# An attention block and a gated feed-forward block in one kernel: the first batch masked by matrix multiplications, the loads and the first stages reordered

## The chip, the cores and the metric

The kernel runs on one core of one Trainium2 chip. The metric is the device time of one execution in microseconds, lower is better. The engines of the core work side by side, each through its own queue of instructions in order: TensorE (PE, matrix multiplications), VectorE (DVE), ScalarE (ACT), GpSimd (POOL) and SyncE (SP, here used only to issue DMAs). DMAs are also issued from POOL's queue and, at the start, from ACT's.

## The reference

```python
def _attn_ref(q, k, v, beacon_k, beacon_v):      # B, H, S, D = 8, 8, 576, 64; 16 beacon rows
    k_all = np.concatenate([beacon_k, k], axis=2)
    v_all = np.concatenate([beacon_v, v], axis=2)
    scores = scale * np.matmul(q, k_all.transpose(0, 1, 3, 2))
    causal[:, Nb:] = np.triu(np.ones((S, S), dtype=bool), k=1)   # beacons are never masked
    scores = np.where(causal, -1000000000.0, scores)
    scores = scores - scores.max(-1, keepdims=True)
    a = np.exp(scores)
    a /= a.sum(-1, keepdims=True) + 1e-09
    return np.matmul(a, v_all)

def _moe_ref(x, w_gate, w_val, w_out):           # x: 4608 x 512; 512 x 1536 twice; 1536 x 512
    g = x @ w_gate
    silu = g * (1.0 / (1.0 + np.exp(-g)))
    val = x @ w_val
    return silu * val @ w_out
```

The attention output of all heads, 4608 rows (tokens) of 512, is the input `x` of the feed-forward block.

## The kernel before

**Attention.** The 8 heads of a batch are worked in 4 pairs. For a pair, K and Q stand transposed in bf16 (`kT`, `qT`). `scores1` and `scores2` each multiply one half of the causal blocks for both heads into two PSUM tiles `s_ps` (8 multiplications of up to 496 columns in `scores2`, 4 in `scores1`), ACT takes the exponential of each tile into a tile `p` in SBUF, and POOL sets the masked entries of `p` to zero with `affine_select` (2 of them in `scores1`, 4 in `scores2`). `pv` multiplies `p` with V for one head (15 small multiplications), and DVE divides by the sum (`rec`, `x`). A pair is thus two score halves and two `pv`, and `pv` of a pair runs one step after its scores.

**Feed-forward.** Tokens go in 9 chunks of 512. A *unit* (`gv_unit`, in the schedule `G`) is 8 multiplications of 512 columns for 128 of the 1536 hidden columns, then tanh on ACT (`th`) and two DVE operations (`u`, `hT`); a chunk has 12 units. The projection of a chunk is 48 multiplications (`out_steps`, in the schedule `F(n)` for n of them): 4 output tiles of 12 each, and after the twelfth DVE copies the tile (`o_sb`) and SP writes it out.

**PSUM.** `big` has three tiles and serves scores and units in turn: whoever asks for a tile waits until the tile three requests earlier has been read (exponential for `s_ps`, `hT` for `gv_ps`). `att` and `outp` are one tile each, for `pv`, transposes and projections.

**Loads and transposes.** Batches below `NPE` = 3 get K and Q as f32 through SP's queue (for the first two pairs of batch 0, Q through ACT's), are cast by DVE (K) and by DVE or ACT (Q), and are transposed on PE (`transpose_pair`, five multiplications and a DVE copy). Later batches are loaded by POOL's queue, whose DMAs cast to bf16 on the way, and transposed by DMA (`dma_transposes`). V and the weights `wg`, `wv` (4 loads each of 384 hidden columns) and `wo` (two loads) come by POOL's casting loads; `pool_todo` hands such loads to POOL in small groups behind the masks of a score half. `x` is transposed on PE for batch 0 (`x_transpose_pair`) and by DMA on SP's queue for the others.

**Order.** It is written by hand and every engine keeps it. Batch 0 has attention alone. Then each pair's scores and `pv` stand between three units, from batch 2 on with 12 projection steps as well: `G scores1 pv F(6) scores2 G pv F(6) G`. Units of chunk j start after batch j+1's second pair has begun. What is left after batch 7 is units and projections alone.

Of the kernel before, what the change touches and what calls it, by code (L numbers as in the profile page):

```python
# [24 lines left out]
NPE = 3  # L25
# [21 lines left out]
def kernel(  # L47
# [30 lines left out]
    o_pool = ctx.enter_context(tc.tile_pool(name="o", bufs=3))  # L78
# [23 lines left out]
    def tiles(t):  # L102
        return t[:].rearrange("p (c h d) -> p c h d", c=NKT, h=H)
# [76 lines left out]
    def transpose_pair(dst, src, n, b, m, pool, tag):  # L180
# [28 lines left out]
    def scores(b, m, which, spec, cols):  # L209
        s = [big.tile([P, 1024], FP32, name="s_ps", tag="big") for _ in range(2)]  # L210
        for t, col, q0, n in spec:
            for hh in range(2):
# [5 lines left out]
                    start=True,  # L218
                    stop=True,
                )  # L220
        for hh in range(2):
# [3 lines left out]
            )  # L225

# [25 lines left out]
    def pv(b, m, hh):  # L252
# [3 lines left out]
        o_ps = att.tile([P, NKT, 68], FP32, name="pv_ps", tag="att")  # L256
# [19 lines left out]
    def x_transpose_pair(b, m, pool, tag):  # L276
# [5 lines left out]
        nc.vector.tensor_copy(xT[:, m, S * b : S * b + S], t_ps[:])  # L282
# [76 lines left out]

    for i in range(2):  # L360
# [10 lines left out]
    make_identity(nc, ident)  # L371
    for load in v_loads(0, 0, 4) + v_loads(0, 4, 8):
# [5 lines left out]

    v1, v2 = v_loads(1, 0, H), v_loads(2, 0, H)
    pool_todo += [[], [], w_loads(0), [], v1[0:3], [], [], v1[3:6]]  # L380
    pool_todo += [w_loads(1), w_loads(2), w_loads(3), [lambda: load_wo(0), lambda: load_wo(1)]]
    pool_todo += [v2[0:3], v2[3:6]]

    steps = [(b, m) for b in range(B) for m in range(NPAIR)]
    end = (B, 0)

    def at(s):
        return steps[s] if 0 <= s < len(steps) else end

    def load_qk_f32(b, h0, h1):  # L390
        load_k_f32(nc.sync, b, h0, h1)
        load_q_f32(nc.sync, b, h0, h1)
# [6 lines left out]
    cast_q(0, 1)  # L399
    load_qk_f32(1, 0, 4)  # L400
# [131 lines left out]
```

## Time and profile before

| | us |
|---|---|
| median of three runs (423.41 to 428.55) | 425.1 |
| the profiled execution | 422.91 |
| its span, first to last instruction | 421.2 |

PE is busy in 377.5 us of the span (90%), DVE in 236.5, ACT in 175.2, POOL in 160.2. A matmul's busy time counts from its start to a modelled end, and the next one starts before that end, so what a multiplication costs in a row is read from start to start and not from the busy figure. The granted TensorE clock is 1.00 of full speed in most of the span and 0.50 in three short stretches.

### The profile page before, as it was taken

How to read it: one execution, taken by the hardware profiler on the slowest of the kernel's cores; microseconds unless marked ns; L12 is line 12 of the kernel's file. 1: busy time of each engine (PE TensorE's matmuls, PEld its weight loads, DVE VectorE, ACT ScalarE, POOL GpSimd, SP SyncE). 2: the span in 40 equal slices, each digit the busy share in tenths (PEclk: the TensorE clock that was granted, in tenths of full speed). 3: DMA queues.
4: the chain of work that ended last, by engine and by line, in shares of the span. 5: the costliest groups of instructions: out<-in, count | busy, mean ns of one | idle time of the engine just before them, and what ended most of it. 6: DMA issues, size and time to landing. Idle time of an engine off the chain costs nothing.

```text
span 421.2 us, 7286 instructions
## 1 busy us (share of the span) xinstructions
PE 377.5 (90%) x2736; PEld 182.2 (43%) x2780; DVE 236.5 (56%) x458; ACT 175.2 (42%) x253; POOL 160.2 (38%) x317
## 2 busy tenths in 40 slices
PE   2756998956998799999999999999999999999996
PEld 1435453422444344444444444444444544444442
DVE  3643766741655455555555555555555664585551
ACT  1536555531445345445555555444555211232210
POOL 8546465390617561846193629261112100000000
PEclk9995998996999999999999999999999999999999
DMA  9999999799868986999499929991310131000012
GB/s 162 152 199 143 188 206 182 84 140 127 74 94 56 170 93 82 94 172 114 64 103 181 125 51 121 150 135 39 75 34 25 41 93 51 25 25 26 25 50 101
DMA packets 169427, 42.89 MB, mean 102 GB/s; under 512 B 159152, under 2 KB 164784, under 8 KB 169392
## 3 DMA queue, kind: packets, MB, share of 16 engines
q0 software_dynamic: 92144, 15.56, 49.0%
q1 hardware_dynamic: 74848, 26.28, 31.6%
q10 hardware_dynamic: 2400, 0.59, 0.7%
q8 instruction: 22, 0.36, 0.4%
q14 instruction: 13, 0.11, 0.1%
HBM read 38.27 MB, written 9.44 MB: 113 GB/s over the span
## 4 chain that ended last, share of the span: by engine, by line
PE 63%; DVE 11%; DMA 11%; another core or an unknown queue 5%; ACT 4%; SPq 2%; issue 2%; ACTq 0%; DVEq 0%
PE gv_ps L301 29%; PE o_ps L330 19%; PE s_ps L214 7%; PE pv_ps L260 6%; DMA q<-in_q_dram 6%; DVE u L312 4%; DVE hT L315 4%; ACT th L310 4%; DMA xT<-x 3%; SPq L289 2%; PE t_ps L185 1%; DMA k<-in_k_dram 1%; DVE qT L186 1%; DVE o_sb L339 1%
## 5 line engine op out<-in xcount | busy, mean ns | idle before, releaser
L312 DVE SCALAR_TENSOR_TENSOR u<-th,gv_ps 128x512 f32<-128x512 f32 x108 | 74.3, 688 | 133.3 <-ACT th L310 133.0
L310 ACT ACTIVATE th<-gv_ps 128x512 f32<-128x512 f32 x108 | 64.4, 597 | 178.9 <-PE gv_ps L301 157.1
L232 POOL TENSOR_SCALAR_AFFINE_SELECT p<-p 128x256 bf16<-128x256 bf16 x192 | 66.6, 380 | 165.7 <-ACT p L223 165.2
L301 PE MATMUL gv_ps<-xT,wg 128*128 128x512 bf16 x418 | 111.6, 383 | 9.8 <-DMA xT<-x 7.8
L223 ACT ACTIVATE p<-s_ps 128x720 bf16<-128x720 f32 (+1 forms) x128 | 103.8, 869 | 37.1 <-PE s_ps L214 36.6
L301 PE MATMUL gv_ps<-xT,wv 128*128 128x512 bf16 x424 | 110.2, 381 | 0.1
L330 PE MATMUL o_ps<-wo,hT 128*128 128x512 bf16 x410 | 101.7, 379 | 1.4 <-DVE o_sb L339 0.4
L315 DVE SCALAR_TENSOR_TENSOR hT<-gv_ps,u 128x512 bf16<-128x512 f32 x108 | 74.7, 691 | 3.7
L214 PE MATMUL s_ps<-qT,kT 64*128 64x96 bf16 (+5 forms) x384 | 48.2, 305 | 18.7 <-ACT p L223 9.1
L301 PEld LDWEIGHTS <-wv 128*128 128x128 bf16 x432 | 42.5, 98 | 51.7 <-issue 1.3
L301 PEld LDWEIGHTS <-wg 128*128 128x128 bf16 x432 | 40.1, 99 | 55.9 <-issue 10.7
L330 PEld LDWEIGHTS <-hT 128*128 128x128 bf16 x432 | 39.0, 98 | 40.4 <-issue 0.6
L260 PEld LDWEIGHTS <-p 128*128 128x128 bf16 x960 | 38.0, 102 | 20.0 <-issue 12.5
L260 PE MATMUL pv_ps<-vb,p 128*128 128x65 bf16 x960 | 43.0, 199 | 1.8 <-DVE kT L186 1.1
L214 PEld LDWEIGHTS <-kT 64*128 64x128 bf16 x384 | 15.8, 98 | 50.8 <-issue 43.9
L114 POOL DMA_DIRECT2D vb<-in_v_dram x45 | 36.8, 831 | 0.3 <-issue 0.2
L269 DVE TENSOR_TENSOR x<-pv_ps,rec 128x320 bf16<-128x320 f32 x64 | 31.5, 492 | 2.2
L339 DVE COPY o_sb<-o_ps 128x512 f32<-128x512 f32 x36 | 24.8, 689 | 11.3 <-PE o_ps L330 11.1
L114 POOL DMA_DIRECT2D kb<-in_k_dram x25 | 21.2, 873 | 0.0
L114 POOL DMA_DIRECT2D qb<-in_q_dram x25 | 21.2, 887 | 0.0
L268 DVE RECIPROCAL rec<-pv_ps 128x5 f32<-128x5 f32 x64 | 12.1, 190 | 6.4 <-PE pv_ps L260 6.2
L185 PE MATMUL t_ps<-ident,kb 128*128 128x128 bf16 (+1 forms) x60 | 7.3, 265 | 6.7 <-DVE kb L169 6.4
(30 smaller groups left out, 74.6 us busy)
## 6 DMA issues: line engine op xcount, KB each, us to landing
out_dram<-o_sb SPq DMA_DIRECT2D x36, 256.0 KB, 2.2
vb<-in_v_dram POOLq DMA_DIRECT2D x21, 128.0 KB, 5.7
q<-in_q_dram SPq DMA_DIRECT2D x20, 128.0 KB, 7.5
qb<-in_q_dram POOLq DMA_DIRECT2D x20, 128.0 KB, 5.5
k<-in_k_dram SPq DMA_DIRECT2D x24, 96.0 KB, 4.9
kb<-in_k_dram POOLq DMA_DIRECT2D x15, 128.0 KB, 4.4
wg<-in_moe_w_gate_dram POOLq DMA_DIRECT2D x4, 384.0 KB, 8.1
wv<-in_moe_w_val_dram POOLq DMA_DIRECT2D x4, 384.0 KB, 10.1
```

What stands on the lines that cost most here:

```text
L114: eng.dma_start(dst[p0 : p0 + n, c, h0:h1, 0:D], src[b, h0:h1, r : r + n, :].rearrange("h j d -> j h d"))
L214: nc.tensor.matmul(s[hh][:, col : col + n], lhsT=kT[b % 2][r, m, P * t : P * t + P], rhs=qT[b % 2][r, m, q0 : q0 + n], start=True, stop=True,)
L223: nc.scalar.activation(p[:, cols[0] : cols[1]], s[hh][:, cols[0] : cols[1]], ACT.Exp, scale=0.125)
L232: nc.gpsimd.affine_select(out=ap, in_=ap, compare_op=ALU.is_ge, fill=0.0, base=base, pattern=pattern, channel_multiplier=-1,)
L260: nc.tensor.matmul(o_ps[:, c, 0 : D + 1], lhsT=pt[2 * (m % 2) + hh][w][:, col : col + P], rhs=vb[b % 2][:, t, h, 0 : D + 1], start=(t == 0 ...
L269: nc.vector.tensor_tensor(out=xs[b][:, :, D * h : D * h + D], in0=o_ps[:, :, 0:D], in1=rec[:].to_broadcast([P, NKT, D]), op=ALU.mult,)
L301: nc.tensor.matmul(ps[:, TOK * half : TOK * half + TOK], lhsT=w[:, kk, P * f : P * f + P], rhs=xT[:, kk, r : r + TOK], start=(kk == 0), st ...
L310: tanh = nc.scalar.activation(th[:], ps[:, 0:TOK], ACT.Tanh, scale=0.5)
L312: nc.vector.scalar_tensor_tensor(out=u[:], in0=th[:], scalar=1.0, in1=ps[:, 0:TOK], op0=ALU.add, op1=ALU.mult)
L315: nc.vector.scalar_tensor_tensor(out=hTs[j][:, f, :], in0=ps[:, TOK:1024], scalar=0.5, in1=u[:], op0=ALU.mult, op1=ALU.mult)
L330: nc.tensor.matmul(st["o"][:], lhsT=hTs[j][:, f, P * i : P * i + P], rhs=wo[:, f, :], start=(f == 0), stop=(f == NF - 1),)
L339: nc.vector.tensor_copy(o_sb[:], st["o"][:])
```

## The change

The diff does six things.

1. In batch 0 the mask is added before the exponential, on PE: a triangular tile `below` of -30000 is multiplied with the identity and added onto the scores, 4 extra multiplications in `scores1` and 6 in `scores2`; POOL's selects are left out there. From batch 1 on they stay.
2. Only the first pair's Q of batch 0, and K of batch 0, are loaded as f32. The rest of Q in batch 0 and all of K and Q of batch 1 come by POOL's casting loads; batch 2 is transposed by DMA (`NPE` = 2).
3. POOL issues 49 loads in a row at the start: Q and V of batch 0, `w` parts 0 and 1, K and Q of batch 1, `w` parts 2 and 3, `wo`, V of batch 1.
4. Eleven multiplications of 512 columns on zeros are run by PE at the start.
5. Chunk 0's 12 units follow batch 0's attention directly, with batch 1's PE transposes between them (their copies on ACT). Batch 1's attention then runs beside the projection of chunk 0; its `x` is transposed on PE too. Chunk 1's first two units are split into parts by `gv_mm` and `gv_act`.
6. From batch 2 on a step is `scores1 pv F(3) scores2 pv F(3) G G G F(6)` (the table `fill` has what batches 2, 3 and 4 leave out of it); DMA transposes are handed out five per step. `o_pool` has 6 buffers in place of 3.

```diff
-NPE = 3
+NPE = 2
-    o_pool = ctx.enter_context(tc.tile_pool(name="o", bufs=3))
+    o_pool = ctx.enter_context(tc.tile_pool(name="o", bufs=6))
...
+        if b == 0:
+
+            for hh in range(2):
+                for t, col, q0, n in spec:
+                    if t or not which:
...
+                        nc.tensor.matmul(
+                            s[hh][:, c0 : c0 + w],
+                            lhsT=below[:],
+                            rhs=ident[:, lo : lo + w],
+                            start=False,
+                            stop=t != 2,
+                        )
...
+            if b == 0:
+                continue
...
+    warm(11, TOK)
...
-    for h in range(0, H, 2):
-        load_k_f32(nc.sync, 0, h, h + 2)
-        load_q_f32(nc.scalar if h < 4 else nc.sync, 0, h, h + 2)
...
+    load_k_f32(nc.sync, 0, 0, 2)
+    load_q_f32(nc.scalar, 0, 0, 2)
+    for m in range(1, NPAIR):
+        load_k_f32(nc.sync, 0, 2 * m, 2 * m + 2)
+    first = q_loads(0, 2, 6) + v_loads(0, 0, 4) + q_loads(0, 6, H) + v_loads(0, 4, H)
+    first += w_loads(0) + w_loads(1) + k_loads(1, 0, H) + q_loads(1, 0, H) + w_loads(2) + w_loads(3)
+    first += [lambda: load_wo(0), lambda: load_wo(1)] + v_loads(1, 0, H)
...
+    for m in range(NPAIR):
+        scores1(0, m)
+        if m < last:
+            transpose_k(0, m + 1, outp, "outp")
+        if m > 1:
+            pv(0, m - 1, 0)
+        scores2(0, m)
+        if m < last:
+            transpose_q(0, m + 1, outp, "outp")
...
+    for _ in range(3):
+        G()
+    for m in range(NPAIR):
+        transpose_k(1, m, outp, "outp", nc.scalar)
+        G()
+        transpose_q(1, m, att, "att", nc.scalar)
+        if m != 1:
+            G()
...
+    fq += out_steps(0, one_bank)
+    for m in range(NPAIR):
+        scores1(1, m)
+        if m >= 2:
+            F(1)
+            x_transpose_pair(1, m - 2, att, "att")
+            F(2)
+        if m:
+            pv(1, m - 1, 0)
+        F(3)
+        scores2(1, m)
+        F(2)
+        if m:
+            pv(1, m - 1, 1)
+        F(1)
...
+    steady = [([], [3], [], [3, g, g, g, 6])] * 4
+    short = ([], [3], [], [3, g, g, g])
+    fill = {
+        2: [([6], [3], [], [3, g, g, g]), ([], [], [], [g, g, g]), ([], [], [], [g, g]), ([], [], [], [g, g])],
+        3: [([], [3], [], [21]), ([], [3], [], [3]), ([], [], [], [g, g, g]), ([], [], [], [g, g, g])],
+        4: [steady[0], short, short, steady[0]],
+    }
...
+                pool_todo += group(loads, 2 if b == 3 else 3)
+            n = fill.get(b, steady)[m]
+            run(n[0])
+            scores1(b, m)
+            if prev:
+                pv(*prev, 0)
+            run(n[1])
+            scores2(b, m)
+            run(n[2])
+            if prev:
+                pv(*prev, 1)
```

On POOL, early in batch 0, the masks of the first score halves stand between V's loads and the first weight loads before the change (`p` are the exponentials, `vb` is V, `wg` and `wv` are the weights):

```order
L114 DMA vb_94<-in_v_dram 128x4x64 x3
L114 DMA vb_94<-in_v_dram 80x4x64
L232 AFFINE_SELECT p_0_100<-p_0_100 128x2x128
L232 AFFINE_SELECT p_1_102<-p_1_102 128x2x128
L232 AFFINE_SELECT p_0_101<-p_0_101 128x2x128
L232 AFFINE_SELECT p_0_101<-p_0_101 128x96
L232 AFFINE_SELECT p_1_103<-p_1_103 128x2x128
L232 AFFINE_SELECT p_1_103<-p_1_103 128x96
L232 AFFINE_SELECT p_2_104<-p_2_104 128x2x128
L232 AFFINE_SELECT p_3_106<-p_3_106 128x2x128
L154 DMA wg<-in_moe_w_gate_dram 128x4x384
L154 DMA wv<-in_moe_w_val_dram 128x4x384
```

After the change POOL's queue holds, behind the second weight part, batch 1's K (`kb`) and Q (`qb`) and the third weight part:

```order
L120 DMA kb_94<-in_beacon_k_dram 16x8x64
L120 DMA kb_94<-in_k_dram 112x8x64
L120 DMA kb_94<-in_k_dram 128x8x64 x3
L120 DMA kb_94<-in_k_dram 80x8x64
L120 DMA qb_92<-in_q_dram 128x8x64 x4
L120 DMA qb_92<-in_q_dram 64x8x64
L161 DMA wg<-in_moe_w_gate_dram 128x4x384
L161 DMA wv<-in_moe_w_val_dram 128x4x384
```

No select stands among the 49 loads, and the third weight part has moved behind two whole tensors of batch 1.

On ACT, where batch 0 ends, batch 1's exponentials (`p0_...`, `p1_...`) and Q casts stood around the first three tanh of chunk 0 (`th`):

```order
L223 ACTIVATE p1_0_101<-s_ps_587 128x720
L223 ACTIVATE p1_1_103<-s_ps_588 128x720
L176 ACTIVATE qb1_91<-q32_88 128x4x128
L176 ACTIVATE qb1_91<-q32_88 64x128
L310 ACTIVATE th_659<-gv_ps_650 128x512
L310 ACTIVATE th_673<-gv_ps_664 128x512
L310 ACTIVATE th_687<-gv_ps_678 128x512
L223 ACTIVATE p0_2_104<-s_ps_692 128x960
L223 ACTIVATE p0_3_106<-s_ps_693 128x960
```

In the changed kernel the last exponentials of batch 0 are followed by three copies of transposed `x`, five tanh, and the first copy of batch 1's transposed K:

```order
L259 ACTIVATE p1_2_106<-s_ps_495 128x720
L259 ACTIVATE p1_3_108<-s_ps_496 128x720
L189 ACTIVATE xT_112<-xt_ps_555 128x576
L189 ACTIVATE xT_112<-xt_ps_584 128x576
L189 ACTIVATE xT_112<-xt_ps_593 128x576
L356 ACTIVATE th_606<-gv_ps_533 128x512
L356 ACTIVATE th_615<-gv_ps_581 128x512
L356 ACTIVATE th_629<-gv_ps_620 128x512
L356 ACTIVATE th_643<-gv_ps_634 128x512
L356 ACTIVATE th_657<-gv_ps_648 128x512
L201 ACTIVATE kT1_100<-t_ps_662 128x592
L356 ACTIVATE th_678<-gv_ps_669 128x512
```

Batch 1's first exponential now comes 20 rows after batch 0's last, behind all twelve tanh of chunk 0.

On DVE, one step of the later batches read before (`rec` and `x` after each `pv`, `o_sb` after a projection tile, `u` and `hT` after each unit):

```order
L268 RECIPROCAL rec_3440<-pv_ps_3424 128x5
L269 TENSOR_TENSOR x_3293<-pv_ps_3424,rec_3440 128x5x64
L339 COPY o_sb_3449<-o_ps_3371 128x512
L312 SCALAR_TENSOR_TENSOR u_3482<-th_3480,gv_ps_3471 128x512
L315 SCALAR_TENSOR_TENSOR hT_3378<-gv_ps_3471,u_3482 128x512
L268 RECIPROCAL rec_3501<-pv_ps_3485 128x5
L269 TENSOR_TENSOR x_3293<-pv_ps_3485,rec_3501 128x5x64
L312 SCALAR_TENSOR_TENSOR u_3522<-th_3520,gv_ps_3511 128x512
L315 SCALAR_TENSOR_TENSOR hT_3378<-gv_ps_3511,u_3522 128x512
L312 SCALAR_TENSOR_TENSOR u_3540<-th_3538,gv_ps_3529 128x512
L315 SCALAR_TENSOR_TENSOR hT_3378<-gv_ps_3529,u_3540 128x512
```

and reads now:

```order
L306 RECIPROCAL rec_3847<-pv_ps_3831 128x5
L307 TENSOR_TENSOR x_3708<-pv_ps_3831,rec_3847 128x5x64
L306 RECIPROCAL rec_3885<-pv_ps_3869 128x5
L307 TENSOR_TENSOR x_3708<-pv_ps_3869,rec_3885 128x5x64
L389 COPY o_sb_3891<-o_ps_3814 128x512
L358 SCALAR_TENSOR_TENSOR u_3906<-th_3904,gv_ps_3895 128x512
L361 SCALAR_TENSOR_TENSOR hT_3894<-gv_ps_3895,u_3906 128x512
L358 SCALAR_TENSOR_TENSOR u_3920<-th_3918,gv_ps_3909 128x512
L361 SCALAR_TENSOR_TENSOR hT_3894<-gv_ps_3909,u_3920 128x512
L358 SCALAR_TENSOR_TENSOR u_3934<-th_3932,gv_ps_3923 128x512
L361 SCALAR_TENSOR_TENSOR hT_3894<-gv_ps_3923,u_3934 128x512
```

Both `pv` come first, the copy of the projection tile stands ahead of the three units, and the last `hT` of a step is followed by the `rec` of the next step's first `pv`.

## Rows read from the trace of the kernel before

**Rows 1.** Busy time by stretch; columns: busy us and count per engine, granted clock, DMA.

```profile
0.00:43.02 43.02, 24.47 (x260) 16.11 (x261) 19.92 (x69) 19.52 (x27) 27.05 (x56) 0.88 1.21 165
43.02:166.12 123.10, 105.48 (x838) 51.48 (x850) 68.91 (x136) 56.82 (x84) 59.69 (x115) 0.96 1.11 127
166.12:330.50 164.38, 161.76 (x1228) 75.28 (x1249) 96.26 (x176) 80.90 (x112) 73.46 (x147) 1.00 0.87 97
330.50:421.20 90.70, 85.83 (x417) 39.35 (x423) 51.41 (x78) 17.91 (x30) 0.00 (x0) 1.00 0.14 48
```

**Rows 2.** Waits of PE from 0 to 166 us; columns: total us, times, longest us.

```profile
PE s_ps L214 <- ACT p L223: 9.1, 6, 6.9
PE gv_ps L301 <- DMA xT<-x: 7.8, 2, 5.9
```

**Rows 3.** Timeline of one step in batch 3; columns: start us, us, engine, line, operation.

```profile
147.12 0.69 DVE L315 SCALAR_TENSOR_TENSOR hT<-gv_ps,u 128x512 bf16<-128x512 f32 x1
147.39 1.03 PE L214 MATMUL s_ps<-qT,kT 64*128 64x496 bf16 x4
148.36 0.63 PE L260 MATMUL pv_ps<-vb,p 128*128 128x65 bf16 x15
148.82 1.46 PE L330 MATMUL o_ps<-wo,hT 128*128 128x512 bf16 x6
...
154.12 1.03 PE L301 MATMUL gv_ps<-xT,wg 128*128 128x512 bf16 x4
...
155.84 1.03 PE L301 MATMUL gv_ps<-xT,wg 128*128 128x512 bf16 x4
...
157.67 1.03 PE L214 MATMUL s_ps<-qT,kT 64*128 64x496 bf16 x4
```

**Rows 4.** Timeline of PE at a first score half with no wait before it.

```profile
104.32 0.58 PE L214 MATMUL s_ps<-qT,kT 64*128 64x496 bf16 x4
104.83 0.63 PE L260 MATMUL pv_ps<-vb,p 128*128 128x65 bf16 x15
```

**Rows 5.** Timeline of batch 0's second and third pair.

```profile
14.58 0.98 PE L214 MATMUL s_ps<-qT,kT 64*128 64x496 bf16 x4 [0.55 <-DVE qT L186]
...
19.98 0.98 PE L214 MATMUL s_ps<-qT,kT 64*128 64x496 bf16 x4 [0.59 <-DVE qT L186]
```

**Rows 6.** Groups by line, 166.12 to 330.5 us; columns: busy us, mean ns, idle before.

```profile
L223 ACT ACTIVATE p<-s_ps 128x960 bf16<-128x960 f32 x32 | 29.3, 968 | 4.0 <-PE s_ps L214 4.0
...
L232 POOL TENSOR_SCALAR_AFFINE_SELECT p<-p 128x256 bf16<-128x256 bf16 x64 | 26.5, 421 | 90.5 <-ACT p L223 90.2
L223 ACT ACTIVATE p<-s_ps 128x720 bf16<-128x720 f32 x32 | 22.9, 768 | 10.2 <-PE s_ps L214 10.2
...
L114 POOL DMA_DIRECT2D vb<-in_v_dram x15 | 12.7, 855 | 0.1
...
L232 POOL TENSOR_SCALAR_AFFINE_SELECT p<-p 128x96 bf16<-128x96 bf16 x32 | 9.0, 283 | 0.0
```

**Rows 7.** Timeline of PE: a `pv` in batch 0, a transpose of Q in batch 1.

```profile
17.77 1.03 PE L260 MATMUL pv_ps<-vb,p 128*128 128x65 bf16 x15
...
53.41 0.52 PE L185 MATMUL t_ps<-ident,qb 128*128 128x128 bf16 x5
```

**Rows 8.** DMA queues from 133 to 137 us; columns: packets, MB, share of 16 engines.

```profile
q0 software_dynamic: 3831, 0.48, 189.6%
```

**Rows 9.** The same from 85 to 97 us, beside DMA transposes.

```profile
q0 software_dynamic: 7577, 0.96, 140.6%
```

**Rows 10.** The same from 46 to 54 us, while weights and f32 rows load.

```profile
q0 software_dynamic: 1546, 1.16, 92.2%
```

**Rows 11.** Timeline of POOL's first loads, and of DVE beside them.

```profile
2.21 3.61 POOL L114 DMA_DIRECT2D vb<-in_v_dram  x5
...
6.39 3.60 POOL L114 DMA_DIRECT2D vb<-in_v_dram  x5
...
6.86 1.04 DVE L178 CAST qb<-q 128x512 bf16<-128x512 f32 x2
```

More of the change, by code (lines that the diff above doesn't have):

```diff
@@ L111, in spans @@
             )
+    loaded = {}
     def rows(eng, dst, src, b, h0, h1, c, p0, r, n):
-        eng.dma_start(
+        if src is not v and src is not beacon_v:
+            key = b, src is not q, c
+            loaded[key] = loaded.get(key, 0) + 1
+        return eng.dma_start(
             dst[p0 : p0 + n, c, h0:h1, 0:D], src[b, h0:h1, r : r + n, :].rearrange("h j d -> j h d")
@@ L357, in F, with warm @@
                 fq.pop(0)()
+    make_identity(nc, ident)
+    nc.gpsimd.memset(below[:], 0.0)
+    nc.gpsimd.affine_select(
+        out=below[:],
+        in_=below[:],
+        compare_op=ALU.is_ge,
+        fill=-30000.0,
+        base=0,
+        pattern=[[-1, P]],
+        channel_multiplier=1,
+    )
+    nc.vector.memset(pt[3][1][:], 0.0)
+    idle = big.tile([P, 1024], FP32, name="idle_ps", tag="big")
+    def warm(n, cols):
+        for _ in range(n):
+            nc.tensor.matmul(
+                idle[:, 0:cols], lhsT=pt[3][1][:, 0:P], rhs=pt[3][1][:, 0:cols], start=True, stop=True
+            )
+    warm(11, TOK)
     for i in range(2):
@@ L376, in group @@
         return [loads[i : i + n] for i in range(0, len(loads), n)]
[L379 to L392, printed above, removed]
+    last = NPAIR - 1
     cast_k(0, 0)
-    cast_q(0, 0)
+    cast_q(0, 0, nc.scalar)
     transpose_k(0, 0, outp, "outp")
@@ new lines @@
+    while gq:
+        G()
+    k2, q2 = k_loads(2, 0, H), q_loads(2, 0, H)
+    for load in k2[0:2] + q2[0:1]:
+        load()
+    for c in range(NKT):
+        pool_todo.append(([k2[c + 2], q2[c + 1]] if c + 1 < NKT else []) + dma_transposes(2)[2 * c : 2 * c + 2])
+    fq += out_steps(0, one_bank)
[13 more added lines that the diff above has]
+        F(1)
@@ new lines @@
+    for load in v_loads(2, 0, H):
+        load()
+    gv_mm(1, 0, 0, last - 1)
+    pv(1, last, 0)
+    F(2)
+    x_transpose_pair(1, last - 1, att, "att")
+    F(2)
+    pv(1, last, 1)
+    gv_mm(1, 1, 0, last - 1)
+    gv_mm(1, 0, last - 1, last)
+    x_transpose_pair(1, last, att, "att")
+    F(2)
+    gv_mm(1, 1, last - 1, last)
+    for f in range(2):
+        gv_mm(1, f, last, KD)
+        gv_act(1, f)
+    gq += [(1, f) for f in range(2, NF)]
+    kq3 = k_loads(3, 0, H) + q_loads(3, 0, H)
@@ new lines, with run @@
+    for load in kq3[0:6]:
+        load()
+    def run(n):
+        for k in n:
+            if k == "G":
+                G()
+            else:
+                F(k)
+    g = "G"
+    steady = [([], [3], [], [3, g, g, g, 6])] * 4
[5 more added lines that the diff above has]
+    }
@@ new lines @@
+    todo = []
+    prev = None
+    for b in range(2, B):
+        for m in range(NPAIR):
+            if m == 2 and b > 2:
+                gq += [(b - 1, f) for f in range(NF)]
+                fq += out_steps(b - 2, one_bank) if b > 3 else []
+            if m == 0 and b + 1 < B:
+                loads = kq3[6:] + [lambda: None] if b == 2 else []
+                if b + 2 < B:
+                    loads += k_loads(b + 2, 0, H) + q_loads(b + 2, 0, H)
+                else:
+                    pool_todo += [[], []]
+                loads += v_loads(b + 1, 0, H)
+                pool_todo += group(loads, 2 if b == 3 else 3)
+            n = fill.get(b, steady)[m]
+            run(n[0])
@@ L481 @@
+            if b == 2 and m == 3:
+                fq += out_steps(1, one_bank)
+            if m == (b == 2) and b + 1 < B:
+                todo = dma_transposes(b + 1)
+            for _ in range(5):
+                if todo:
+                    todo.pop(0)()
+            prev = (b, m)
     G()
```

176 lines of the change are left out of this document (76 added, 100 removed).

## The prediction

> **What bounds the kernel now.** I read the busy time by stretch first [rows 1]. From 166.12 us on PE is the bound: 161.76 of 164.38 us in batches 4 to 7, and behind them only units and projections. Before that it is not: 24.47 of 43.02 us until the first unit, 105.48 of 123.10 us in the next stretch. In those 166 us PE stands idle for 36 us, and part of the rest runs at half clock (0.88 and 0.96 granted). The waits say for whom [rows 2]: 9.1 us for exponentials, 6.9 of them one wait in which batch 1's f32 Q had not come, and 7.8 us for the transposed `x`. So the early part is held by loads and by the order, the late part by PE's own work. In the late part I then read one step [rows 3]: it lasts 157.67 - 147.39 = 10.28 us (164.38 / 16 = 10.27 over the sixteen steps, [rows 1]), of which a unit is 155.84 - 154.12 = 1.72, one 512-column multiplication so 0.215, a `pv` 148.82 - 148.36 = 0.46. The first score half takes 148.36 - 147.39 = 0.97 there, against 104.83 - 104.32 = 0.51 where it need not wait [rows 4]: its second tile is the one of the unit just before the last, and its `hT` ends only at 147.12 + 0.69 = 147.81.
>
> **How I sum.** At 166.12 us the kernel before has 78 units, 354 projection multiplications and 16 pairs to go (counted in the code). The changed kernel has the same left when batch 4 begins. So I need the time T at which that is, and what the rest costs. Prices, all from rows: a unit 1.72; a pair 2 x 0.46 for `pv`, 0.51 for the first score half and an estimated 0.40 for the second (720 columns against 960), 1.83; a pair's exponentials 2 x 0.97 + 2 x 0.77 = 3.47 on ACT; its masks 4 x 0.42 + 2 x 0.28 = 2.25 on POOL; a load of a tensor's 128 rows 0.86 on POOL [rows 6]; a PE transpose of a pair 0.52 [rows 7].
>
> **Batch 0 (until units 0 and 1 are done): 32 us.** Batch 0's second pair begins at 14.58 and its third at 19.98 [rows 5], 5.40 us apart, while ACT alone would need 3.47. Removed: POOL's masks and DVE's Q casts, which lie on the way from one pair to the next. Added: 10 mask multiplications a pair. No row shows them; nothing is the lower bound, since ACT's 3.47 can cover them, and 10 x 0.52 / 5 = 1.0 us, the transposes' price, the upper. I take them inside a pace of 4.5 us, between 3.47 and 5.40. K's f32 loads are first in SP's queue as before, so the second pair stays at 14.5; the fourth begins at 23.5, its exponentials end at 27, and its `pv`, three `x` transposes and what is left of two units take 5 us more.
> What the row shows of the loads that move to POOL: five loads took 3.61 us before DVE's casts begin and 3.60 beside them, 0.72 each [rows 11]. The Trainium skill, page "SBUF — State Buffer", section "SBUF: two separate sides", says that a DMA issued from GpSimd is held up while DVE runs a fast copy or cast, because its descriptors cannot be written. By that rule the four K casts of batch 0 would each hold a load up, by 0.4 to 0.5 us, and the sum would be 2 us higher; the row speaks against it here.
>
> **Chunk 0: until 55.7.** 10 units are 17.2, eight transposes at most 4.2, together 21 us, so 53. Are the weights there? POOL needs 0.65 to 0.72 for each of the 22 half loads ahead [rows 11], so `w` parts 0 and 1 are issued from 17 us on. Weight packets (768 B, 1024 a part pair) passed at 1546 / 8 = 193 a us with f32 rows beside them [rows 10]; without those I take 230. Small packets (one row of 64 values; 9344 for batch 1's K and Q) passed at 3831 / 4 = 958 a us alone [rows 8] and 7577 / 12 = 631 beside transposes [rows 9]. So parts 0 and 1 are in by 28, K and Q by 38, part 2 by 42.5, part 3 by 47, `wo` by 55, V of batch 1 by 60. Unit 6 is due at 39.8 and waits 2.7 us for part 2; the later units are then late enough.
>
> **Batch 1 beside projection 0: until 82.** PE's work is 4 x 1.83, 36 x 0.215, four `x` transposes of 0.52 and two units of chunk 1: 20.6 us. The first `pv` would come at 59 and waits for V until 60.5. Behind that POOL is late: 8 loads x 0.86 stand between the masks of the first two pairs, 9.0 + 6.9 = 16 us of POOL work that can only begin with the exponentials; I walked it step by step and get 4 us of waits of `pv` for masks. 20.6 + 1.5 + 4 = 26.1, say 26.3 with seams.
>
> **Batch 2: until 112, batch 3: until 142.** Batch 2 has 12 projection steps, 10 units and 4 pairs on PE, 27.2 us, and on POOL 23 loads and 24 masks, 19.8 + 9.0 = 28.8, after 12 further loads (10 us) queued in front. POOL is the bound by a little, and in three steps the second score half waits about 1 us for the last unit's tile, since no projection stands between: 30. Batch 3: 30 x 0.215 + 6 x 1.72 + 4 x 1.83 = 24.1 on PE, 17 x 0.86 + 9.0 = 23.6 on POOL behind what batch 2 left; waits for masks of 0.7 and 2.5, for a tile 1.1, seams 1: 30. T = 142, against 166.1: **24 us won**. With every wait of mine at zero T is 125 (32, 53, 73.6, 100.8, 124.9).
>
> **The rest.** In the new step six projection multiplications (1.3 us) stand between the third unit and the next scores, so the tile is free in time: 0.46 of the 10.27 go, and up to 0.24 of seams (10.27 less 3 x 1.72, 12 x 0.215, 1.83 and 0.46). The stall could only move to `o_sb`; but the projection tile ends with the second `F(3)`, ahead of three units, and its copy hides under 5.2 us of them. I take 9.72, between 9.57 and 10.27: 16 x 0.55 = 8.8 less 1.4 for three short steps of batch 4, whose tile wait stays at 0.45. The last stretch is the same work, 90.70. 164.4 - 7.4 + 90.7 = 247.7. Span 142 + 247.7 = 389.7; with the 1.7 us around the span (422.91 - 421.2) 391.4, against 422.91. The profiled execution is 0.5% below the median of 425.1, so I say **392** for the median.
>
> Costed at nothing: the eleven first multiplications (PE has nothing else to do before the first K comes; at half clock they are 11 x 0.43 = 4.7 us), the ACT copies of batch 1 (ACT has one tanh per unit there), the DMA transposes of batch 2 on SP (needed at 83, issued from 64 on), the six `o_sb` buffers, which cover output writes queued behind transposes that wait for loads.
>
> **Rivals.**
> - *My waits do not happen* (0.14). For it: every one is a few us and hangs on a rate. Against: POOL's load of work is real. Half of the 17 us between T = 125 and 142 gone: **383**.
> - *Loads hold the early part* (0.14). If small packets pass at 631 a us, as beside transposes [rows 9], batch 1's K and Q take 5 us more, its V 2.6, and the 37,500 packets of eight tensors of batches 2 to 4 take 59 instead of 39 us, of which about half shows: T = 154, **404**.
> - *The clock does not hold in batch 0* (0.09). In batch 0 the fifteen multiplications of a `pv` took 1.03 us [rows 7], in the late part 0.46 from start to start: half clock. The change puts eleven multiplications first, but PE then waits for the second pair's K from 9.3 to 11.6. Two transposes, a `pv` and the masks at double price on each of three links are 1.5 us a pair: **397**. The Trainium skill, page "TensorE: Matmul & The Clock Gate", section "HAM oscillation — how this bites in real kernels", describes matmul bursts between DMA waits that each start slow again; whether batch 0's gaps do that no row here shows.
> - *The wait in the late step only moves* (0.07), to another tile or to `o_sb`: 0.53 us a step stay, **400**.
> - *Slower: POOL becomes the bound* (0.04). Between 55 and 142 us POOL has 60 loads (52 us) and 27 us of masks, 79 of 87 us. Should a load take twice as long on POOL's queue once 49 are outstanding, that is 52 us more, and PE waits for the masks: T = 186 and **436**. Of these, 44 show, past the 8 us that POOL has free. It is slower than before from 1.55 us a load on (60 x 0.69 = 33 + 8). Against it: loads took 0.72 and 0.86 in full and empty stretches alike [rows 6, 11].
> That the mask is not on PE, or the order not the one written, can be excluded from the instruction order.
>
> **How the numbers follow.** My own case, 384 to 400, has 0.52. For 8 in 10 the range goes from **378** (most waits gone) to **410** (loads hold, and a little more): the POOL rival and the far ends of two others, about 0.15, stay out. Faster by over 2% means below 416.6, about what a measurement of this kernel can tell from no change: all cases but the slower one and the far end of the load rival give that, 0.91; within 2% 0.06; slower by over 2% 0.03.
>
> **What would show it.** In the profile after: batch 4's first scores near 142 us; the late step at 9.7 us, with a first score half of 0.5; one wait for `wv` or `wg` near unit 6 and one for V near 60; `pv` waiting for POOL's masks in batches 1 to 3 and POOL without a gap from 60 to 115. A late step of 10.2, or batch 4 after 150, would prove me wrong.

## The result, and the profile after

| | before | after |
|---|---|---|
| median, us | 424.64 | 394.38 (393.57 to 395.57) |
| ratio, 95% interval | | 0.9275 (0.9207 to 0.9343) |
| the profiled execution, its span | 422.91, 421.2 [rows 1] | 395.57, 393.9 |

The forecast was 392 us, between 378 and 410. Busy time of the changed kernel by stretch (columns as in rows 1), cut where its stages begin: the first whole unit, batch 1, its end, the first scores of batches 3 and 4, and 90.70 us before the end:

```profile
0.00:33.01 33.01, 26.95 (x295) 16.22 (x296) 14.95 (x53) 17.71 (x23) 27.07 (x44) 0.84 1.42 148
33.01:54.50 21.49, 20.51 (x122) 9.97 (x121) 14.95 (x22) 10.36 (x18) 11.26 (x15) 1.00 1.45 179
54.50:79.81 25.31, 22.06 (x242) 11.31 (x241) 10.64 (x25) 13.71 (x18) 22.04 (x42) 1.00 1.83 146
79.81:111.78 31.97, 29.98 (x231) 13.95 (x231) 19.19 (x35) 18.90 (x27) 27.72 (x49) 1.00 1.93 145
111.78:141.46 29.68, 26.62 (x247) 12.78 (x247) 14.96 (x31) 16.39 (x22) 22.62 (x43) 1.00 1.62 144
141.46:303.20 161.74, 160.79 (x1274) 75.74 (x1274) 101.38 (x183) 80.62 (x114) 65.44 (x137) 1.00 0.85 91
303.20:393.90 90.70, 85.72 (x409) 38.75 (x407) 49.59 (x75) 17.32 (x29) 0.00 (x0) 1.00 0.15 51
```

The two profiled executions differ by 27.3 us in span, the medians by 30.3: the profiled one of the changed kernel is 1.2 us above its median, that of the kernel before 1.7 below.

Batch 4 begins at 141.46 us; before, the comparable point was 166.12. What is left then takes 252.4 us against 255.1, with one unit more in it (78 against 77: of PE's 864 weight loads for units, 8 a unit, 615 came behind 166.12 in the kernel before). Counted with the same work left, at 1.72 us for that unit, 22.9 of the 27.3 us come from the early part and 4.4 from the late one.

The waits of PE from 0 to 160 us (total, times, longest), to be held against rows 2:

```profile
PE pv_ps L298 <- POOL p L270: 2.2, 2, 1.2
PE s_ps L232 <- ACT p L259: 1.8, 5, 0.4
PE t_ps L198 <- DVE kb L176: 1.7, 1, 1.7
PE pv_ps L298 <- DVE x L307: 1.6, 8, 0.4
...
PE o_ps L380 <- DVE o_sb L389: 1.5, 2, 0.8
...
PE gv_ps L343 <- DMA wv<-in_moe_w_val_dram: 0.9, 1, 0.9
```

The wait of 6.9 us for batch 1's f32 Q and the 7.8 us for transposed `x` are gone, and no wait that this list shows is longer than 1.7 us. One late step in PE's timeline, which answers to rows 3:

```profile
190.27 0.58 PE L232 MATMUL s_ps<-qT,kT 64*128 64x496 bf16 x4
190.78 0.63 PE L298 MATMUL pv_ps<-vb,p 128*128 128x65 bf16 x15
191.25 0.81 PE L380 MATMUL o_ps<-wo,hT 128*128 128x512 bf16 x3
191.99 0.48 PE L232 MATMUL s_ps<-qT,kT 64*128 64x336 bf16 x8
192.41 0.62 PE L298 MATMUL pv_ps<-vb,p 128*128 128x65 bf16 x15
...
198.70 1.46 PE L380 MATMUL o_ps<-wo,hT 128*128 128x512 bf16 x6
200.09 0.58 PE L232 MATMUL s_ps<-qT,kT 64*128 64x496 bf16 x4
```

It lasts 200.09 - 190.27 = 9.82 us against 10.27, its first score half 0.51 against 0.97.

### The profile page after: what moved, and what is told of

It is laid out like the page before. It is cut to its first block, busy times and chain, and to the rows that moved or that the text cites. A ratio compares the mean times of both kernels' runs of the same rounds, so it can differ in the third digit from the quotient of the medians.

```text
span 393.9 us, 7274 instructions
## 1 busy us (share of the span) xinstructions
PE 372.6 (95%) x2811; PEld 178.7 (45%) x2811; DVE 225.7 (57%) x420; ACT 175.0 (44%) x250; POOL 176.2 (45%) x327
## 4 chain that ended last, share of the span: by engine, by line
PE 71%; POOL 8%; DMA 7%; DVE 7%; issue 2%; ACT 2%; SPq 1%; POOLq 0%; DVEq 0%; ACTq 0%
PE gv_ps L343 40%; PE o_ps L380 21%; PE pv_ps L298 6%; PE s_ps L232 4%; DMA wo<-in_moe_w_out_dram 4%; POOL qb L120 3%; DMA wv<-in_moe_w_val_dram 3%; POOL vb L120 2%; DVE u L358 2%; ACT th L356 2%; DVE hT L361 2%; DVE x L307 2%; DVE o_sb L389 1%; DMA xT<-x 1%; SPq L327 1%
## 5 line engine op out<-in xcount | busy, mean ns | idle before, releaser
L259 ACT ACTIVATE p<-s_ps 128x720 bf16<-128x720 f32 (+1 forms) x128 | 102.3, 871 | 40.1 <-PE s_ps L232 31.1
L343 PE MATMUL gv_ps<-xT,wv 128*128 128x512 bf16 x432 | 112.2, 379 | 0.9 <-DMA wv<-in_moe_w_val_dram 0.9
L380 PE MATMUL o_ps<-wo,hT 128*128 128x512 bf16 x432 | 109.7, 379 | 2.7 <-DVE o_sb L389 2.6
L270 POOL TENSOR_SCALAR_AFFINE_SELECT p<-p 128x256 bf16<-128x256 bf16 (+1 forms) x168 | 57.5, 374 | 98.8 <-ACT p L259 98.4
L298 PE MATMUL pv_ps<-vb,p 128*128 128x65 bf16 x960 | 40.6, 193 | 5.1 <-POOL p L270 2.2
L232 PE MATMUL s_ps<-qT,kT 64*128 64x80 bf16 (+5 forms) x384 | 41.2, 291 | 4.1 <-ACT p L259 1.8
L298 PEld LDWEIGHTS <-p 128*128 128x128 bf16 x960 | 33.8, 97 | 21.6 <-issue 11.4
L120 POOL DMA_DIRECT2D qb<-in_q_dram x45 | 37.0, 839 | 2.3 <-DMA wg<-in_moe_w_gate_dram 1.9
L120 POOL DMA_DIRECT2D kb<-in_k_dram x35 | 29.8, 865 | 6.3 <-DMA vb<-in_beacon_v_dram 2.9
L198 PE MATMUL t_ps<-ident,kb 128*128 128x128 bf16 (+1 forms) x40 | 4.2, 239 | 2.6 <-DVE kb L176 1.7
```

The lines of the kernel that those rows point to most:

```text
L120: return eng.dma_start(dst[p0 : p0 + n, c, h0:h1, 0:D], src[b, h0:h1, r : r + n, :].rearrange("h j d -> j h d"))
L232: nc.tensor.matmul(s[hh][:, col : col + n], lhsT=kT[b % 2][r, m, P * t : P * t + P], rhs=qT[b % 2][r, m, q0 : q0 + n],  start=b > 0 or not ...
L259: nc.scalar.activation(p[:, cols[0] : cols[1]], s[hh][:, cols[0] : cols[1]], ACT.Exp, scale=0.125)
L270: nc.gpsimd.affine_select(out=ap, in_=ap, compare_op=ALU.is_ge, fill=0.0, base=base, pattern=pattern, channel_multiplier=-1,)
L298: nc.tensor.matmul(o_ps[:, c, 0 : D + 1], lhsT=pt[2 * (m % 2) + hh][w][:, col : col + P], rhs=vb[b % 2][:, t, h, 0 : D + 1], start=(t == 0 ...
L343: nc.tensor.matmul(gvs[f][:, TOK * half : TOK * half + TOK], lhsT=w[:, kk, P * f : P * f + P], rhs=xT[:, kk, r : r + TOK], start=(kk == 0) ...
```

## The experiments

My theory: the early gain needs three things together (mask on PE, loads in a row, chunk 0 ahead of batch 1); the late order is worth about 6 us by itself; POOL is near its bound from 57 to 141 us; TensorE's clock in batch 0 decides little. What was measured, medians in us and ratios to the kernel before in the same job:

| kernel | mask on PE | loads | early order | late order | us | ratio, 95% |
|---|---|---|---|---|---|---|
| mask alone | yes | old | old | old | 423.02 | 1.000 (0.998 to 1.003) |
| late order alone | no | old | old | new | 417.27 | 0.986 (0.983 to 0.989) |
| mask and loads | yes | new | old | old | 439.36 | 1.039 (1.034 to 1.043) |
| all but the mask, loads in a row | no | new | new | new | 425.78 (one run) | |
| all but the mask, loads spread | no | spread | new | new | 410.91 | 0.971 (0.967 to 0.974) |
| all but the late order | yes | new | new | old | 400.71 | 0.944 (0.941 to 0.948) |

The table has a gap: no run has the new early order with the old f32 loads. That the new loads are needed too is therefore argued from the waits for f32 Q that the traces show, and not shown by a run.

### The kernel before with the mask on PE alone

```diff
+        if b == 0:
+            for hh in range(2):
...
+                        nc.tensor.matmul(s[hh][:, c0 : c0 + w], lhsT=below[:], rhs=ident[:, lo : lo + w], ...)
...
+            if b == 0:
+                continue
```

> The kernel before, with only the mask of batch 0 moved to PE as in the change; loads, order and casts as before. Theory (the early gain needs the loads and the order: batch 0 gets shorter, but the wait for batch 1's f32 Q takes its place): 421 to 424 us, and that wait longer than 6.9 us. Rival (the mask on PE carries the early gain by itself): 412 or less.

423.02 us, no change. The wait for batch 1's Q shrank from 6.88 to 1.82 us, and one of 5.67 us stands where batch 2's f32 Q is late. DVE's and PE's timelines in this kernel (in brackets the idle time ahead and what ended it):

```profile
20.18 0.55 DVE L179 CAST qb<-q 128x512 bf16<-128x512 f32 x2 [4.44 <-DMA q<-in_q_dram]
...
30.36 0.58 PE L215 MATMUL s_ps<-qT,kT 64*128 64x496 bf16 x4 [0.82 <-DVE qT L187]
...
34.03 0.47 PE L215 MATMUL s_ps<-qT,kT 64*128 64x336 bf16 x7 [1.82 <-ACT p L241]
...
70.05 0.57 PE L215 MATMUL s_ps<-qT,kT 64*128 64x496 bf16 x1 [5.67 <-DVE qT L187]
```

So the theory's total holds, but not its way there. Batch 0 did not get shorter: its fourth pair begins at 30.36 us instead of 25.71, since DVE waits 4.44 and 2.94 us for batch 0's own f32 Q. POOL, free of masks, issues the first weight loads at 10.18 instead of 17.85 us; that these took the DMA engines' time from Q is likely, but no run separates it. And the long wait ahead is for batch 2's Q, not batch 1's.

### Mask and loads of the change, order of before

```diff
-    for load in v_loads(0, 0, 4) + v_loads(0, 4, 8):
+    first = q_loads(0, 2, 6) + v_loads(0, 0, 4) + q_loads(0, 6, H) + v_loads(0, 4, H)
+    first += w_loads(0) + w_loads(1) + k_loads(1, 0, H) + q_loads(1, 0, H) + w_loads(2) + w_loads(3)
+    first += [lambda: load_wo(0), lambda: load_wo(1)] + v_loads(1, 0, H)
+    for load in first:
         load()
...
+        if b == 1:        # in load_qk_f32, cast_k and cast_q
+            return
```

> The kernel before with the mask of batch 0 on PE and the loads of the change (Q of batch 0 behind the first pair and K and Q of batch 1 by casting loads, the 49 first loads in a row, no casts for them), but PE's order as before: batch 1's attention right behind batch 0's, chunk 0 after it. Theory (loads and order only pay together): batch 1's K comes at 34 to 40 us while PE has no unit to run, and its masks stand behind the 49 loads, whose last is issued at about 55: 418 to 430 us, with waits for batch 1's K or Q and for POOL's masks of 10 us and more. Rival (mask and loads carry the early gain, the order is not needed): 405 or less.

439.36 us, slower than before, and 9 above my upper end. PE's waits in this kernel (total, times, longest):

```profile
PE t_ps L190 <- DMA kb<-in_k_dram: 11.9, 5, 5.9
PE gv_ps L325 <- DMA xT<-x: 8.6, 2, 4.6
...
PE pv_ps L284 <- DMA vb<-in_v_dram: 5.2, 4, 3.9
```

The five waits for batch 1's K end between 34.53 and 41.66 us: in the changed kernel chunk 0's units fill that time. I expected POOL's masks as the second wait; it was V, last of the 49 loads, and the DMA transposes of `x` took more. The rival (mask and loads carry the gain) falls: it is 34 us off.

### Batch 0 masked on POOL, all else changed

Loads in a row as in the changed kernel; the ten extra multiplications a pair are left out and POOL's selects are back:

```diff
-            if b == 0:
-                continue
```

> The changed kernel with batch 0 masked by POOL's selects again, all loads in their new order. Theory (the mask left POOL because 52 loads now stand in its queue ahead of any select, the last of them issued near 57 us): the first pv of batch 0 comes at about 57 instead of 18 us, and the kernel takes about 430 us, slower than the one before the change. Rival (batch 0 is paced by ACT's exponentials, and the place of the mask is worth the 9 us of POOL work at most): 394 to 400.

425.78 us, one run, which can't be told from the 424.15 of the kernel before in that job (421.79 to 427.25); so "slower than before" is not shown. PE's timeline at the first `pv`:

```profile
46.47 0.46 PE L296 MATMUL pv_ps<-vb,p 128*128 128x65 bf16 x5 [31.37 <-POOL p L268]
```

PE waits 31.4 us for it, since the masks stand behind the 49 loads; I had expected it near 57 us. Batch 4 begins at 171.22. In the second version the loads are handed out between the score halves:

```diff
-    for load in first:
+    for load in q_loads(0, 2, 6) + v_loads(0, 0, 4):
         load()
+    pool_todo += [q_loads(0, 6, H), v_loads(0, 4, H)[0:3], v_loads(0, 4, H)[3:6] + w_loads(0), w_loads(1) + k1[0:3]]
+    pool_todo += [k1[3:6] + q1[0:2], q1[2:5] + w_loads(2), w_loads(3) + wo2]
+    pool_todo.append(v_loads(1, 0, H))
```

> The changed kernel with batch 0 masked on POOL again, but with the 49 first loads not in a row: 11 ahead, the others handed out behind batch 0's eight score halves, so no mask stands behind all of them. Theory (POOL then has 9 us of masks among 35 us of loads, and batch 0 waits for them): 398 to 406 us, pv of batch 0 waiting for POOL's masks, batch 4 starting 4 to 10 us later. Rival (the mask's engine does not matter, only the order of POOL's queue did): 393 to 396.

410.91 us, 5 over my upper end. Its PE timeline and its stretches (columns as in rows 1):

```profile
22.89 0.73 PE L296 MATMUL pv_ps<-vb,p 128*128 128x65 bf16 x10 [3.08 <-POOL p L268]
...
33.54 0.73 PE L296 MATMUL pv_ps<-vb,p 128*128 128x65 bf16 x10 [5.20 <-POOL p L268]
...
0.00:35.00 35.00, 21.05 (x181) 11.42 (x182) 12.17 (x46) 13.63 (x17) 32.60 (x61) 0.68 1.27 135
35.00:60.00 25.00, 19.08 (x134) 10.65 (x138) 10.84 (x20) 9.21 (x15) 15.19 (x24) 0.77 1.65 180
```

Four waits for masks come to 14.0 us, and the granted clock of these stretches is down: 0.68 and 0.77, against 0.85 and 1.00 for the same stretches of the changed kernel. Batch 1 begins at 69.43 instead of 54.50, batch 4 at 156.05, 14.6 us later. POOL is busy in 32.6 of the first 35 us, so loads and masks together fill it. The mask on PE is thus worth 16.5 us against the better of the two load orders tried with masks on POOL, and nothing in the kernel before: it pays here because it frees POOL to issue 49 loads. Other ways to spread the loads were not tried.

### Twice as many load instructions

```diff
+        for g0, g1 in ((h0, h1),) if b < 2 else ((h0, h0 + 4), (h0 + 4, h1)):
+            one = eng.dma_start(dst[p0 : p0 + n, c, g0:g1, 0:D], src[b, g0:g1, r : r + n, :].rearrange(...))
```

> The changed kernel with each load of batches 2 to 7 issued as two of four heads: the same bytes and packets, twice as many instructions on POOL. Theory (POOL is close to being the bound from 57 to 141 us): 51 loads there become 102 of about 0.7 us (the price of a four-head load in batch 0) in place of 0.86, some 28 us more, against about 18 us that POOL is idle there; batch 4 starts 8 to 20 us later, 402 to 415 us, pv waiting for POOL. Rival (POOL has room, or the waits stay beside PE's work): 394 to 397.

414.64 us, ratio 0.9794 (0.9764 to 0.9824); batch 4 begins at 159.11, 17.7 us later, both within the theory's ranges. POOL's timeline at the loads of V of batch 2, ten of four heads here and five of eight in the changed kernel (last two lines), and three stretches of this one:

```profile
77.80 7.18 POOL L121 DMA_DIRECT2D vb<-in_v_dram  x10
84.89 1.11 POOL L121 DMA_DIRECT2D kb<-in_beacon_k_dram  x2
...
74.49 4.23 POOL L120 DMA_DIRECT2D vb<-in_v_dram  x5
78.67 0.58 POOL L120 DMA_DIRECT2D kb<-in_beacon_k_dram  x1
```

```profile
85.00:115.00 30.00, 23.66 (x160) 11.16 (x162) 13.12 (x25) 13.77 (x19) 30.00 (x52) 0.89 1.68 117
115.00:145.00 30.00, 22.14 (x205) 10.78 (x207) 10.92 (x23) 13.79 (x18) 29.38 (x56) 0.89 1.26 101
145.00:165.00 20.00, 18.96 (x160) 9.18 (x160) 12.13 (x23) 10.95 (x17) 20.00 (x39) 1.00 1.33 115
```

POOL has no gap from 85 to 115 us and next to none until 145, `pv` waits 14.7 us for it, and PE is at half clock for a part (0.50 granted from 100 to 105 us). So POOL's room in the changed kernel is real but small. From start to start a load of four heads costs (84.89 - 77.80) / 10 = 0.71 us, one of eight (78.67 - 74.49) / 5 = 0.84. So two halves cost 0.58 more than one whole, some 30 us for 51 loads; the theory had 28.

### The late order, undone and by itself

The changed kernel with the steps of batches 4 to 7 in the old order:

```diff
-    steady = [([], [3], [], [3, g, g, g, 6])] * 4
+    steady = [([g], [6], [g], [6, g])] * 4
-    short = ([], [3], [], [3, g, g, g])
+    short = ([g], [3], [g], [3, g])
```

> The changed kernel with the old order in the steps of batches 4 to 7: a unit, scores1, pv, six projections, scores2, a unit, pv, six projections, a unit. Theory (the late gain is the first score half, which no longer waits for the tile of the unit before last): the step goes from 9.82 back to about 10.27 us, the first score half from 0.51 to 0.97, and 12 full steps and 4 of batch 4 give 5 to 6 us: about 400. Rival (all of the gain is made before batch 4, and in the late steps a wait only changes its place): 394, no change.

400.71 us, 6.3 above the changed kernel, as the theory had it. Its batch 4 begins at 141.99 and its last step at 295.19, 153.2 us, against 141.46 and 288.44, 147.0, in the changed kernel: the 6.2 us lie in these steps. The first half waits again (PE's timeline):

```profile
201.47 1.03 PE L232 MATMUL s_ps<-qT,kT 64*128 64x496 bf16 x4
202.44 0.63 PE L298 MATMUL pv_ps<-vb,p 128*128 128x65 bf16 x15
...
205.15 1.02 PE L343 MATMUL gv_ps<-xT,wg 128*128 128x512 bf16 x4 [0.37 <-DVE hT L361]
```

The same order put into the kernel before:

```diff
-            G()
+            old = b < 4
+            if old:
+                G()
...
-            F(6)
+            F(6 if old else 3)
...
+            if not old:
+                G()
+                G()
+                F(6)
```

> The kernel before, with only the steps of batches 4 to 7 put into the new order (scores, pv, F3, scores, pv, F3, three units, F6). Theory (the late order is worth about 6 us whatever stands ahead of it): 418 us, 417 to 420, and a first score half of about 0.5 us instead of 0.97 in these steps. Rival (its worth hangs on the changed early part or on the table's other steps): 423 to 425.

417.27 us, 6.0 below the kernel before in the same job (423.29). So this part gives the same with either early part. Its trace, of an execution of 1297 us, is not read; that its first score half takes 0.5 us is therefore not shown.

### TensorE's clock in batch 0

Without the eleven first multiplications, and with twenty:

```diff
-    warm(11, TOK)
```

> The changed kernel without the eleven multiplications on zeros at the start. Theory (the clock falls at 7.5 us anyway while PE waits, and batch 0 runs at half clock until 17.8): the same within 1 us, 394. Rival (they hold the clock up through a part of batch 0): 397 to 399, with batch 0's third pair beginning 2 us later or more.

```diff
-    warm(11, TOK)
+    warm(20, TOK)
```

> The changed kernel with twenty instead of eleven multiplications on zeros, so that PE is busy until the first K is cast at about 7 us. Theory (what lets the clock fall is the idle time from 5.4 to 7.2 us): the granted clock stays at 1.00, a pv in batch 0 takes 0.46 from start to start, and the time is 392, 2 us less. Rival (the waits between batch 0's pairs let it fall as well, or batch 0 is paced by exponentials and data and hides the clock): 394, no change.

394.58 and 394.40 us: no change by either. PE's timeline, in the changed kernel from the first transpose on:

```profile
7.17 0.73 PE L198 MATMUL t_ps<-ident,kb 128*128 128x128 bf16 x5 [1.74 <-DVE kb L176]
...
9.04 0.99 PE L232 MATMUL s_ps<-qT,kT 64*128 64x496 bf16 x4 [0.55 <-DVE qT L203]
9.96 0.58 PE L250 MATMUL s_ps<-ident,below 128*128 128x112 bf16 x4
```

with twenty:

```profile
9.55 0.58 PE L232 MATMUL s_ps<-qT,kT 64*128 64x496 bf16 x4 [0.56 <-DVE qT L203]
10.06 0.38 PE L250 MATMUL s_ps<-ident,below 128*128 128x112 bf16 x4
```

and without any, at the first and the second pair:

```profile
8.49 0.98 PE L232 MATMUL s_ps<-qT,kT 64*128 64x496 bf16 x4 [0.55 <-DVE qT L203]
...
13.39 0.58 PE L232 MATMUL s_ps<-qT,kT 64*128 64x496 bf16 x4 [0.55 <-DVE qT L203]
```

With twenty, PE is busy until the transposes of the first K follow at 8.21 us, with no wait ahead of them, and four scores take 0.51 instead of 0.92 us. The fourth pair begins at 22.74 instead of 24.46 and batch 1 at 52.51 instead of 54.50; the two spans differ by 1.6 us, less than executions of one kernel differ (393.68 to 396.73). So the granted clock did what the theory of the twenty said, and the 2 us did not show in the median: its rival holds.

Without any, the first four scores take 0.92 us too, half speed (though the profile's clock column reads 1.00 there), but those of the second pair only 0.51, and the third pair begins at 17.55 us, 1.8 earlier than in the changed kernel. So in these two executions the eleven multiplications kept nothing up, and the rival of this run fails by its own sign. Nor does the fall come each time: in the second trace of the next experiment, whose kernel starts with the same eleven, K comes after 0.94 us of waiting instead of 1.74, 1.00 is granted all along, and the four pairs begin at 8.13, 11.76, 15.92 and 20.91 us.

### Four waits of the changed kernel taken away

```diff
-    two_banks = [(outp, "outp"), (att, "att")]
+    two_banks = [(att, "att"), (outp, "outp")]
...
-        2: [([6], [3], [], [3, g, g, g]), ...
-        3: [([], [3], [], [21]), ([], [3], [], [3]), ([], [], [], [g, g, g]), ([], [], [], [g, g, g])],
+        2: [([6], [3], [], [g, g, g, 3]), ...
+        3: [([], [3], [], [9]), ([], [3], [], [9]), ([], [], [], [g, g, g, 3]), ([], [], [], [g, g, g, 3])],
```

The loads of batch 2, and those handed out during batch 3, are regrouped as the expectation says.

> The changed kernel with four waits taken away that its trace shows: the first tile of the last projections comes from the other PSUM bank (0.8 us), batch 2's K and Q loads stand one or two behind each score half instead of three ahead of batch 1's masks (1.2 us), batch 3's 30 projection steps go 12, 12, 3, 3 with three of them behind the units (o_sb 0.8, two third-unit waits of about 0.9), and its loads leave out the half after which pv waited 1.0 us; batch 2's first step has its F3 behind the units (0.5). Theory (PE bounds and each wait goes): 388.5 us, 387 to 391. Rival (other waits take their places): 393.5 to 395.

393.79 us (0.9296, 0.9258 to 0.9333). Run again:

> The kernel with four waits taken away once more, for a profile at full clock (its first profiled execution ran at a granted clock of 0.85 throughout). It measured 393.8 us where 388.5 were expected. Theory now (the waits are gone, but the stages end where loads or DMA transposes let them): batch 4 begins at 139 to 141 us and PE shows a new wait of 2 to 4 us ahead of it. Rival (the times of batches 2 to 7 are as computed, and the first 60 us are longer in this kernel's runs): batch 4 begins 5 us earlier than its batch 1 would have it.

395.50 us (0.9337, 0.9287 to 0.9386). Neither differs from the changed kernel; the first rival holds. Batch 1 begins at 53.12, 1.4 us earlier, which is not the edit's doing but batch 0's at full clock; batch 4 begins at 140.90, only 0.6 earlier. PE's timeline shows the first pair and what took the places:

```profile
8.13 0.58 PE L232 MATMUL s_ps<-qT,kT 64*128 64x496 bf16 x4 [0.56 <-DVE qT L203]
...
80.05 0.37 PE L232 MATMUL s_ps<-qT,kT 64*128 64x464 bf16 x2 [0.80 <-DMA qT<-qb]
...
91.08 0.62 PE L298 MATMUL pv_ps<-vb,p 128*128 128x65 bf16 x15 [0.62 <-DVE x L307]
...
125.03 0.59 PE L343 MATMUL gv_ps<-xT,wg 128*128 128x512 bf16 x1 [1.85 <-DMA xT<-x]
```

The loads that I had moved back made batch 2's transposes late (0.80). Of the 27 projection multiplications that stood between the issue of the DMA transposes of `x` and batch 3's units, 6 now stand behind units; with them and two waits gone, PE came to the units before `x` was there (1.85). So of my second theory "a new wait ahead of batch 4" holds, at 1.9 us just under its range, and the rival's 5 us of gain is not there.

## Why the prediction was right, step by step

- **Batch 0, 32: measured 33.01.** The mask multiplications cost 0.37 and 0.53 us a pair at half clock (9.96 to 10.33 and 12.09 to 12.62 us), 0.9 together, near my upper end of 1.0; at full clock, with twenty first multiplications, 0.23 and 0.31. The pairs begin at 9.04, 13.97, 19.36 and 24.46, 5.1 us apart instead of 4.5; with twenty first multiplications 4.4, in the mended kernel's trace 4.3. The difference is the clock rival, which did happen in this execution.
- **The clock rival, 397.** Its mechanism is in the trace: PE ends its first multiplications, waits 1.74 us for K, and from 7.54 to 17.77 it has half the clock granted, 1.00 after that:

```profile
7.54:17.77 10.24, 9.04 (x69) 5.35 (x69) 3.84 (x10) 5.36 (x7) 10.07 (x16) 0.51 1.46 141
```

  The size was wrong: not 5 us but at most 2, and nothing in the medians. The Trainium skill's section "HAM oscillation — how this bites in real kernels" (page "TensorE: Matmul & The Clock Gate") has matmul bursts that start slow again behind a DMA wait. This trace agrees, with 0.92 us for four scores behind the wait for K; the mended kernel's does not, with 0.51 behind its wait of 0.94 us.
- **Chunk 0 until 55.7: 54.50.** The wait for `w` part 2 is where I put it, in unit 6, but 0.9 us, not 2.7.
- **Batch 1 until 82: 79.81.** The six projections that follow count with batch 2 in the forecast. So 25.3 us against 26.3, and made up otherwise: no wait for V, 1.2 us for masks instead of 4, and in their place 0.7 for `o_sb`, 0.6 for a tile at the first `scores2`, and seams.
- **Batch 2 until 112, batch 3 until 142: 111.78 and 141.46.** The steps without projections lose time, and more than the forecast's 1 us: one lasts 8.57 us (89.53 to 98.10) for 3 x 1.72 + 1.83 = 6.99 of work. That POOL would have no gap from 60 to 115 did not come true. It was busy 27.7 of 32.0 us in batch 2 and `pv` did not wait for it there; PE was busy 30.0. The half loads show how close POOL is.
- **T = 142: 141.46, in part by luck.** Held against their forecasts, the five stages until then missed by +1.0, -2.2, -1.0, +2.0 and -0.3 us, which cancel.
- **The rest, 247.7: measured 252.4.** This is the term that missed most, by 4.7 us, all of the miss in the sum (393.9 against 389.7). One unit, 1.72, I had counted wrong: before, a unit had already run ahead of 166.12 us, so 77 were left there and not 78. Twelve steps at 9.82 instead of 9.72 are 1.2. The last 1.8 I do not separate: the first and last step of batch 4 last 10.5 us each, because no projections stand behind the units ahead of them, and there are two late waits for `o_sb`, 1.1 us together.
- **392 for the median: 394.38.** The forecast's own rule, a profiled execution 0.5% below its median, would have made 391.4 into 393.4. The rule did not hold: here the profiled execution, 395.57, lies above.
- **The late order, 7.4 won: 6.0 to 6.3** by the two experiments, 4.4 between the traces before and after, which hold batch 4's short steps and the `o_sb` waits as well. Neither of the possible new stalls came. The rival "the wait only moves" is wrong for these steps, and right for the steps without projections between their halves: in the mended kernel such a step got its first half down to 0.51 us and lost 0.41 and 0.62 right behind it.
- **POOL becomes the bound, 436.** Loads cost 0.84 to 0.89 us from start to start with 49 and more issued, so it did not. Its arithmetic holds: with 0.58 us more for each of 51 loads, less the 8 us that POOL has free, it gives some 22 us more, and the half loads cost 20.3.
- **Loads hold, 404:** no wait in batches 2 and 3 was for a load.

A page's rule weighed ahead, that a fast DVE copy holds a GpSimd-issued DMA up (the Trainium skill, "SBUF — State Buffer", section "SBUF: two separate sides"), is not seen here either: in the changed kernel groups of five loads took 3.75, 3.64, 3.51 and 3.61 us, the first beside DVE's memsets and the others beside K casts, against 3.61 without [rows 11].

## What to carry to other kernels

Moving work off an engine pays by what its queue can then do: the mask on PE was worth nothing in the old order, where batch 0 then waited for its f32 Q, and 16.5 us where POOL had 49 loads to issue. Give the time in which a load is under way a stage of its own work, and test parts in pairs, since mask plus loads without the order was 16 us slower than neither. In a step with three PSUM tiles, keep short work of another kind between the last unit and the next scores, and between the score halves too.

## What was not expected of the hardware

POOL's issues do not run ahead without limit. Its timeline in the changed kernel (in brackets the idle time and what ended it):

```profile
47.18 0.73 POOL L120 DMA_DIRECT2D vb<-in_v_dram  x1 [1.39 <-DVE u L358]
51.80 0.53 POOL L120 DMA_DIRECT2D kb<-in_beacon_k_dram  x1 [3.89 <-DMA wo<-in_moe_w_out_dram]
55.28 0.83 POOL L120 DMA_DIRECT2D kb<-in_k_dram  x1 [2.94 <-DMA vb<-in_beacon_v_dram]
```

From 25 to 56 us ten such waits stand ahead of POOL's loads, and eight of them end, by the trace, with the landing of the load eight places before, counted from the first of the 49. The longest, 3.89 us, is behind the two loads of `wo`. The masks of batch 1's first pair stand behind these loads and have two more between them, and `pv` waits 1.22 us there; in the mended kernel, with one load fewer ahead of them and one fewer between, it does not wait. I had let POOL issue freely.

The price of a load on POOL goes far more by the instruction than by the bytes: 0.71 us from start to start for four heads, 0.84 for eight. (A group's mean in the profile misleads here: 909 ns for 36 loads of four heads, which were busy for 27.4 us in all, 0.76 each, since neighbours overlap.) And where PE waits again and again, the clock takes part of the next work too: with half loads PE waits 4.87 us for masks until 98.81 us, and from 100 to 105 only 0.50 is granted; from 85 to 145 us it is 0.89, where the changed kernel has 1.00.
